# Key blocks of 96 partitions whose overlaps and memory rows all come by DMA

## The chip, the core and the metric

The kernel runs on one core of a Trainium2 chip. The metric is the device time of one execution in microseconds (us), from the first to the last instruction. Five engines work side by side and are joined by semaphores: TensorE (PE, matrix products), VectorE (DVE), ScalarE (ACT), GpSimd (POOL) and SyncE (SP, which only issues transfers). Transfers (DMA) run on 16 engines that are shared by all queues. SBUF is the on-chip memory of 128 partitions, PSUM the memory into which TensorE writes.

## The reference: what is computed

Two stages in one launch. First, chunked attention over 4 batches x 8 heads x 768 positions x 64. A chunk of 32 queries sees 16 keys to its left, its own 32 and 8 to its right, and 8 memory rows that each head has besides:

```python
chunk, left_ctx, right_ctx = (32, 16, 8)
for c in range(nc):
    c_start, c_end = c * chunk, (c + 1) * chunk          # names shortened
    l_start, r_end = max(0, c_start - left_ctx), min(S, c_end + right_ctx)
    k_full = concat([mem_k, k[:, :, l_start:r_end]])
    v_full = concat([mem_v, v[:, :, l_start:r_end]])
    a = softmax(q_c @ k_full.T / sqrt(64))
    out[:, :, c_start:c_end] = a @ v_full
```

Then, on x of shape 4 x 768 x 512 (the heads side by side):

```python
u  = x + real(fft(fft(x, axis=1), axis=2))
un = (u - mean) / sqrt(var + 1e-6)
out = u + relu(un @ w_ch1) @ w_ch2          # 512 -> 2048 -> 512
```

## The kernel before

The work is cut into 16 *pairs* of heads (n = 0 to 15), four to a batch. For each pair: q and k are loaded, cast to bf16, transposed on TensorE (trq, trk) and copied out of PSUM by ScalarE (qT, kTb); scores, exponentials and the product with v follow in two halves g. Two chunks of 32 queries are taken together, so a *block* is 64 queries wide, and a bias per half (mbias) masks the keys that a chunk must not see. The softmax needs no sum of its own: v has a 65th column of ones, and column 64 of the product is the denominator.

A block's keys span 16 + 64 + 8 rows and the 8 memory rows. Before, a block had 128 partitions: 64 keys (0 to 63), the memory rows (64 to 71), unused rows (72 to 95) and, at 96 to 127, the first 32 keys of the next block, which hold what the overlap needs. In kTb this comes for free, because blocks stand 96 columns apart and a block of 128 columns reads into the next one. For v, GpSimd copies the rows inside SBUF.

```python
    NV = 6
    va = [spool.tile([P, NB, 66], FP32, name=f"va{i}") for i in range(NV)]      # NB = 13 blocks

    def e_load_v(n, hh):                        # one head
        b, pr = seq[n]
        v1 = va[(2 * n + hh) % NV]
        vb = v[b, 2 * pr + hh]
        nc.sync.dma_start(v1[16:64, 0:NT, 0:D],                # NT = 12
                          bass.AP(tensor=vb.tensor, offset=vb.offset,
                                  ap=[[D, 48], [64 * D, NT], [1, D]]))
        nc.sync.dma_start(v1[0:16, 1:NB, 0:D],
                          bass.AP(tensor=vb.tensor, offset=vb.offset + 48 * D,
                                  ap=[[D, 16], [64 * D, NT], [1, D]]))
        nc.sync.dma_start(v1[64:72, 0:NT, 0:D],
                          mem_v[b, 2 * pr + hh].unsqueeze(1).to_broadcast([NMEM, NT, D]))

    def e_overlap(n, hh):
        v1 = va[(2 * n + hh) % NV]
        nc.gpsimd.tensor_copy(v1[96:128, 0:NT, 0:D + 1], v1[0:32, 1:NB, 0:D + 1])

    def e_kT(n):
        nc.scalar.copy(
            strided(kTb[n % NKT], 0, [[BS, NB], [8, 8], [1, RB]]),           # BS = 96
            strided(tr_of.pop((n, 1)), 0, [[8, NB], [1, 8], [KP, RB]]))      # KP = 104

    def e_scores(n, g):        # ... cut
                nc.tensor.matmul(sc[:, hh, t6, :], kT[r0:r0 + 64, t * BS:t * BS + P],
                                 qT[r0:r0 + 64, ts(t, 64)], start=True, stop=True,
                                 tile_position=(r0, 0))

    def e_exp(n, g):           # ... cut
            nc.scalar.activation(e1[:, :, :, ts(half, 32)], sc[:, :, 0:6, ts(half, 32)],
                                 AFT.Exp, bias=mbias[:, half:half + 1], scale=1.0 / math.sqrt(D))

    def e_values(n, g):        # ... cut
                    nc.tensor.matmul(xa[64 * half:64 * half + 64, st, hh, 0:65],
                                     e1[:, hh, t6, :], v1[:, 6 * g + t6, 0:65],
                                     start=True, stop=True)
```

At the start, six va, three kf and two kTb tiles are cleared: one kf on VectorE, one va and both kTb on GpSimd, the rest on ScalarE.

After the attention of a batch comes its Fourier part: sums and differences on VectorE (zy, pq, ff), a split into two fp16 halves (hi on ScalarE, lo on VectorE), products with cosine and sine tables (ps, pm), sums and statistics on VectorE. Then the MLP: ph = first matrix, hT = relu on ScalarE, pc = second matrix, osb on VectorE, and a store. The Fourier part of one batch and the attention of the next run beside the MLP of the batch before.

In which order each engine takes these steps is decided in the kernel itself, before anything is issued. A small planner (class Plan) gets every step with an engine, a guessed cost, its predecessors and the buffers that it takes and gives back, plays the schedule through with these guesses and emits the steps in the order found. A guess thus never changes what is computed, but it can change the order of the queues:

```python
        lq = add("SP", 0.35, lambda: e_load_q(n), take=("qf",), moved=1.3)
        lk = add("SP", 0.35, lambda: e_load_k(n), [t_clear["kf", n] if n < NS else None],
                 take=("kf",), moved=1.3)
        lv = [add("SP", 1.1, lambda hh=hh: e_load_v(n, hh),
                  [t_ones[2 * n + hh] if 2 * n < NV else None],
                  take=("va",) if hh == 0 else (), moved=2.3) for hh in range(2)]
        # batch 0: casts on VectorE, the others: on GpSimd
        ov = [add("POOL", 0.84, lambda hh=hh: e_overlap(n, hh), [lv[hh]]) for hh in range(2)]
        # ...
            v_ = add("PE", 0.85, lambda g=g: e_values(n, g), [x_] + ov, take=(tag,),
                     give=("e1", "va") if g == 1 else ("e1",))
```

The weights w_ch1 and w_ch2 are loaded through GpSimd's queue, in order behind its casts and copies.

Of the kernel before, what the change touches and what calls it, by code (L numbers as in the profile page):

```python
# [10 lines left out]
FP32 = mybir.dt.float32  # L11
# [6 lines left out]
LEFT = 16  # L18
RIGHT = 8
NMEM = 8  # L20
BIGM = 800.0

# [89 lines left out]
def kernel(  # L112
# [22 lines left out]
    KP = QP + 8  # L135
    NB = KP // 8
    BS = 96
# [18 lines left out]
    NV = 6  # L156
    va = [spool.tile([P, NB, 66], FP32, name=f"va{i}") for i in range(NV)]
    NKT = 2
    kTb = [spool.tile([P, NB * BS], BF16, name=f"kTb{i}") for i in range(NKT)]

    HP = H // 2
    seq = [(b, pr) for b in range(B) for pr in (0, 2, 1, 3)]

    plan = Plan(dict(qf=NS, kf=NS, va=NV // 2, kTb=NKT, qb=1, kb=1, qT=2, tr=1, sc=1, xa=1, e1=3,
# [6 lines left out]
    mkf = cpool.tile([P, 2, D], FP32)  # L171
    mkb = cpool.tile([P, 2 * D], BF16)
# [11 lines left out]
    ident = cpool.tile([P, P], FP32)  # L184
# [25 lines left out]
    def e_masks():  # L210
        nc.gpsimd.memset(mbias, NEG)
        nc.gpsimd.memset(mbias[0:72, :], 0.0)
        nc.gpsimd.memset(mbias[96:128, 1:2], 0.0)
        nc.gpsimd.affine_select(out=mbias[0:64, 0:1], in_=mbias[0:64, 0:1],
                                compare_op=ALU.is_ge, fill=NEG,
                                base=CHUNK + LEFT + RIGHT - 1, pattern=[[0, 1]],
                                channel_multiplier=-1)
        nc.gpsimd.memset(mbias[0:32, 1:2], NEG)
        nc.gpsimd.affine_select(out=mbias[96:128, 1:2], in_=mbias[96:128, 1:2],
                                compare_op=ALU.is_ge, fill=NEG, base=RIGHT + LEFT - 1,  # L220
                                pattern=[[0, 1]], channel_multiplier=-1)
# [5 lines left out]
    def e_clear_act(t):  # L227
        flat = t if len(t.shape) == 2 else t.rearrange("p a b -> p (a b)")
        nc.scalar.copy(flat, zero[0:flat.shape[0]].to_broadcast(list(flat.shape)))

    def e_ones(i):
        nc.vector.memset(va[i][0:72, :, 64:65], 1.0)
        nc.vector.memset(va[i][0:16, 0, 64:65], 0.0)
        nc.vector.memset(va[i][0:64, NB - 1, 64:65], 0.0)
        nc.vector.memset(va[i][0:16, NB - 1, 64:65], 1.0)
# [8 lines left out]
    def e_load_q(n):  # L244
        b, pr = seq[n]
        nc.sync.dma_start(qf[n % NS],
                          q[b, 2 * pr:2 * pr + 2].rearrange("h (p j) d -> p h (j d)", j=RB))

    def e_load_k(n):
        b, pr = seq[n]  # L250
        nc.sync.dma_start(kf[n % NS][2:2 + QP],
                          k[b, 2 * pr:2 * pr + 2].rearrange("h (p j) d -> p h (j d)", j=RB))

    def e_load_v(n, hh):
        b, pr = seq[n]
        v1 = va[(2 * n + hh) % NV]
        vb = v[b, 2 * pr + hh]
        nc.sync.dma_start(v1[16:64, 0:NT, 0:D],
                          bass.AP(tensor=vb.tensor, offset=vb.offset,
                                  ap=[[D, 48], [64 * D, NT], [1, D]]))  # L260
        nc.sync.dma_start(v1[0:16, 1:NB, 0:D],  # L261
                          bass.AP(tensor=vb.tensor, offset=vb.offset + 48 * D,
                                  ap=[[D, 16], [64 * D, NT], [1, D]]))
        nc.sync.dma_start(v1[64:72, 0:NT, 0:D],
                          mem_v[b, 2 * pr + hh].unsqueeze(1).to_broadcast([NMEM, NT, D]))


    qT_of, kT_of, qb_of, kb_of, tr_of, e1_of, sc_of, xa_of, xs = ({} for _ in range(9))
    cp_q = "p h (j d) -> p h j d"
    cp_b = "p j h d -> p h j d"  # L270

    def e_cast_q(n, eng):
        qb_of[n] = apool.tile([QP, RB, 2, D], BF16, tag="qb", bufs=1, name="qb")
        eng.tensor_copy(qb_of[n].rearrange(cp_b), qf[n % NS].rearrange(cp_q, j=RB))  # L274

    def e_cast_k(n, eng):
        kb_of[n] = apool.tile([KP, RB, 2, D], BF16, tag="kb", bufs=1, name="kb")
        eng.tensor_copy(kb_of[n].rearrange(cp_b), kf[n % NS].rearrange(cp_q, j=RB))

    def e_overlap(n, hh):  # L280
        v1 = va[(2 * n + hh) % NV]
        nc.gpsimd.tensor_copy(v1[96:128, 0:NT, 0:D + 1], v1[0:32, 1:NB, 0:D + 1])  # L282
# [24 lines left out]
    def e_mkT(n):  # L307
        b, pr = seq[n]
        nc.vector.tensor_copy(
            kTb[n % NKT].rearrange("p (b c) -> p b c", b=NB)[:, 0:NT, 64:72],  # L310
            mkT[:, b * HP + pr, :].unsqueeze(1).to_broadcast([P, NT, NMEM]))

    def e_kT(n):
        nc.scalar.copy(  # L314
            strided(kTb[n % NKT], 0, [[BS, NB], [8, 8], [1, RB]]),
            strided(tr_of.pop((n, 1)), 0, [[8, NB], [1, 8], [KP, RB]]))

    def e_scores(n, g):
        qT, kT = qT_of[n], kTb[n % NKT]
        sc_of[n, g] = sc = aps.tile([P, 2, 8, 64], FP32, tag="sc", bufs=1, name="sc")  # L320
        for t6 in range(6):
            t = 6 * g + t6
            for hh in range(2):
                r0 = 64 * hh
                nc.tensor.matmul(sc[:, hh, t6, :], kT[r0:r0 + 64, t * BS:t * BS + P],  # L325
                                 qT[r0:r0 + 64, ts(t, 64)], start=True, stop=True,
                                 tile_position=(r0, 0))

    def e_exp(n, g):
        sc = sc_of.pop((n, g))  # L330
        e1_of[n, g] = e1 = apool.tile([P, 2, 6, 64], FP32, tag="e1", bufs=3, name="e1")
        for half in range(2):
            nc.scalar.activation(e1[:, :, :, ts(half, 32)], sc[:, :, 0:6, ts(half, 32)],  # L333
                                 AFT.Exp, bias=mbias[:, half:half + 1],
                                 scale=1.0 / math.sqrt(D))

    def e_values(n, g):
# [6 lines left out]
        for st in range(3):  # L344
            for hh in range(2):
                v1 = va[(2 * n + hh) % NV]
                for half in range(2):
                    t6 = 2 * st + half
                    nc.tensor.matmul(xa[64 * half:64 * half + 64, st, hh, 0:65],  # L349
                                     e1[:, hh, t6, :], v1[:, 6 * g + t6, 0:65],  # L350
                                     start=True, stop=True)
# [174 lines left out]
    t_clear = {}  # L526
    t_clear["kf", 0] = add("DVE", 0.9, lambda: nc.vector.memset(kf[0], 0.0))
    t_id = add("POOL", 0.5, lambda: make_identity(nc, ident))
    t_clear["va", 0] = add("ACT", 1.0, lambda: e_clear_act(va[0]), [t_zero])
    t_clear["va", 1] = add("POOL", 0.9, lambda: nc.gpsimd.memset(va[1], 0.0))  # L530
    t_scales = add("DVE", 0.2, e_scales, [t_iota])
    t_idb = add("DVE", 0.25, lambda: nc.vector.tensor_copy(ident_b, ident), [t_id])
    t_masks = add("POOL", 0.9, e_masks)
    for i in range(1, NS):
        t_clear["kf", i] = add("ACT", 1.15, lambda i=i: e_clear_act(kf[i]), [t_zero])
        for m in (2 * i, 2 * i + 1):
            t_clear["va", m] = add("ACT", 1.0, lambda m=m: e_clear_act(va[m]), [t_zero])
    for i in range(NKT):
        t_clear["kTb", i] = add("POOL", 1.15, lambda i=i: nc.gpsimd.memset(kTb[i], 0.0))
    t_ones = {i: add("DVE", 0.3, lambda i=i: e_ones(i), [t_clear["va", i]]) for i in range(NV)}  # L540
# [27 lines left out]
    def attention(n):  # L568
        b, pr = seq[n]
        lq = add("SP", 0.35, lambda: e_load_q(n), take=("qf",), moved=1.3)  # L570
        lk = add("SP", 0.35, lambda: e_load_k(n), [t_clear["kf", n] if n < NS else None],
                 take=("kf",), moved=1.3)
        lv = [add("SP", 1.1, lambda hh=hh: e_load_v(n, hh),
                  [t_ones[2 * n + hh] if 2 * n < NV else None],
                  take=("va",) if hh == 0 else (), moved=2.3) for hh in range(2)]
        first = b == 0
        ce, cn, cc = (nc.vector, "DVE", 0.68) if first else (nc.gpsimd, "POOL", 1.04)
        cq = add(cn, cc, lambda: e_cast_q(n, ce), [lq], take=("qb",), give=("qf",))
        ck = add(cn, cc, lambda: e_cast_k(n, ce), [lk], take=("kb",), give=("kf",))
        ov = [add("POOL", 0.84, lambda hh=hh: e_overlap(n, hh), [lv[hh]]) for hh in range(2)]  # L580
# [4 lines left out]
        mk = add("DVE", 0.2, lambda: e_mkT(n), [t_mkT, t_clear["kTb", n] if n < NKT else None],  # L585
                 take=("kTb",))
        ek = add("ACT", 0.85, lambda: e_kT(n), [tk, mk], give=(ktag,))
        for g in range(2):
# [5 lines left out]
            v_ = add("PE", 0.85, lambda g=g: e_values(n, g), [x_] + ov, take=(tag,),  # L594
# [192 lines left out]
```

The softmax here doesn't subtract the row's maximum and nothing guards it: scores larger than these inputs give would overflow.

## Time and profile before

| | |
|---|---|
| time, median of 3 runs | 342.35 us (341.04 to 342.84) |
| span of the profiled execution | 339.3 us |
| moved by DMA | 33.02 MB in 51839 packets, 40032 of them under 512 bytes |
| share of GpSimd | 80.6 us busy, 24% of the span |

The profile page gives busy times by engine, the span in slices, the DMA queues, the chain of work that ended last (followed back from the last instruction to what released each step), and groups of equal instructions. In a group, "L282 POOL COPY va<-va ... x32 | 36.2, 1138 | 50.0 <-DMA" would read: line 282, on GpSimd, 32 instructions, 36.2 us in all, 1138 ns each; before them the engine stood idle for 50.0 us, most of it ended by a DMA. A table of windows gives, for each stretch of time, how long each engine was busy (with the number of instructions), the clock that TensorE was granted, the share of the 16 DMA engines' time in which packets were under way (it can pass 1, as packets overlap) and the rate in GB/s.

The DMA queue of SyncE carries the loads of q, k and v, and the transposes of un:

```
q1 hardware_dynamic: 45376, 22.03, 36.9%
```

that is packets, MB and the time of the packets as a share of 16 engines' span.

### The profile page before, as it was taken

To read this page: it belongs to the slowest core of one execution; us is meant where nothing else is said; L and a number is where in the kernel's file an instruction comes from. 1 tells how busy PE (TensorE), PEld (TensorE's weight loads), DVE (VectorE), ACT (ScalarE), POOL (GpSimd) and SP (SyncE) were. 2 spreads that over 40 slices of the span, in tenths; PEclk is the share of its full clock that TensorE was granted. 3 is DMA by queue.
4 is the path that set the end of the run, shared out by engine and by line. 5 is a ranking of instruction groups with operands and counts; after the bars stand their busy time and mean duration, and the time that the engine had idled before them with its cause. 6 is when DMAs were issued, how large, how long until landed. Compare 5 with 4: busy or idle time off the path is not lost.

```text
span 339.3 us, 6789 instructions
## 1 busy us (share of the span) xinstructions
PE 289.6 (85%) x2761; PEld 185.4 (55%) x2761; DVE 183.2 (54%) x356; ACT 168.9 (50%) x297; POOL 80.6 (24%) x89
## 2 busy tenths in 40 slices
PE   0678647969998886969999997898999999999995
PEld 0467536847565565547755654574445454554542
DVE  6964498868089899599773469782010100101001
ACT  7554885557637448676633623335436053250620
POOL 5634594224342637252001200000010000000000
PEclk9999999879999999898999999599999999999999
DMA  7999999999407785692063100000340100201001
GB/s 157 214 183 162 168 229 203 220 173 178 72 3 152 131 182 136 183 201 36 0 110 101 31 3 2 31 31 33 68 119 2 62 31 2 93 0 64 31 32 63
DMA packets 51839, 33.02 MB, mean 97 GB/s; under 512 B 40032, under 2 KB 42080, under 8 KB 51808
## 3 DMA queue, kind: packets, MB, share of 16 engines
q1 hardware_dynamic: 45376, 22.03, 36.9%
q0 software_dynamic: 2688, 4.19, 6.7%
q10 hardware_dynamic: 3744, 6.36, 4.9%
q8 instruction: 22, 0.36, 0.5%
q14 instruction: 9, 0.07, 0.1%
HBM read 28.11 MB, written 6.29 MB: 101 GB/s over the span
## 4 chain that ended last, share of the span: by engine, by line
PE 62%; DVE 14%; DMA 9%; ACT 4%; POOL 3%; issue 3%; SPq 3%; ACTq 0%; POOLq 0%
PE ph L496 23%; PE pc L510 22%; DMA qf<-in_q_dram 8%; PE xa L349 7%; PE pm L445 4%; PE ps L413 2%; SPq L261 2%; DVE zy L373 2%; DVE lo L403 2%; PE sc L325 1%; DVE ff L390 1%; DVE st L457 1%; DVE pq L381 1%; ACT e L333 1%; DVE pq L380 1%
## 5 line engine op out<-in xcount | busy, mean ns | idle before, releaser
L503 ACT ACTIVATE hT<-ph 128x384 f16<-128x384 f32 x128 | 61.2, 492 | 70.5 <-PE ph L496 70.3
L496 PE MATMUL ph<-unT,w_sb 128*128 128x384 f16 x512 | 92.2, 327 | 2.4 <-ACT hT L503 1.8
L510 PE MATMUL pc<-w_sb,hT 128*128 128x512 f16 x384 | 87.3, 382 | 0.0
L516 DVE SCALAR_TENSOR_TENSOR osb<-pc,rstd,xsb 128x512 f32<-128x512 f32 x24 | 17.8, 746 | 98.3 <-PE pc L510 98.3
L496 PEld LDWEIGHTS <-w_sb 128*128 128x128 f16 x512 | 48.3, 97 | 37.9 <-issue 8.2
L510 PEld LDWEIGHTS <-hT 128*128 128x128 f16 x384 | 37.2, 98 | 42.4 <-issue 1.5
L282 POOL COPY va<-va 32x780 f32<-32x780 f32 x32 | 36.2, 1138 | 50.0 <-DMA va<-in_v_dram 37.9
L333 ACT ACTIVATE e<-sc,mbias 128x384 f32<-128x384 f32 x64 | 33.7, 579 | 20.0 <-PE sc L325 19.1
L349 PE MATMUL xa<-va,e 128*64 128x65 f32 x768 | 35.4, 253 | 8.6 <-ACT e L333 3.7
L349 PEld LDWEIGHTS xa<-va,e 128*64 128x64 f32 x768 | 30.6, 162 | 15.7 <-issue 7.7
L463 ACT ACTIVATE un<-xsb,mu_s 128x512 f16<-128x512 f32 x24 | 17.3, 722 | 24.5 <-DVE mu_s L458 15.8
L359 DVE RECIPROCAL zs<-xa 128x6 f32<-128x6 f32 x32 | 6.1, 190 | 34.5 <-PE xa L349 34.3
L325 PE MATMUL sc<-qT,kTb 64*128 64x64 bf16 x384 | 12.8, 207 | 12.6 <-ACT kTb L314 11.0
L484 POOL TENSOR_SCALAR rstd<-mu_s 128x6 f32<-128x6 f32 x4 | 1.0, 244 | 89.7 <-DVE osb L516 83.7
L413 PE MATMUL ps<-cosS,lo 128*128 128x193 f16 (+1 forms) x72 | 16.6, 285 | 4.6 <-DVE lo L403 4.5
L274 POOL CAST qb<-qf 96x1024 bf16<-96x1024 f32 x12 | 14.9, 1242 | 20.8 <-DMA qf<-in_q_dram 11.9
L413 PE MATMUL ps<-cosS,hi 128*128 128x193 f16 (+1 forms) x72 | 16.7, 285 | 3.4 <-DVE ff L390 3.2
L425 ACT CAST up<-ps 128x386 f16<-128x386 f32 x16 | 9.7, 605 | 19.4 <-PE ps L413 17.8
L325 PEld LDWEIGHTS <-kTb 64*128 64x128 bf16 x384 | 8.8, 104 | 18.5 <-ACT kTb L314 12.3
L360 DVE TENSOR_TENSOR xsb<-xa,zs 128x384 f32<-128x384 f32 x32 | 17.8, 557 | 1.1
L398 ACT CAST hi<-ff 128x768 f16<-128x768 f32 x16 | 13.2, 832 | 10.1 <-DVE ff L390 9.9
L403 DVE TENSOR_TENSOR lo<-ff,hi 128x768 f16<-128x768 f32 x16 | 16.8, 1063 | 2.2 <-ACT hi L398 2.1
(90 smaller groups left out, 356.2 us busy)
## 6 DMA issues: line engine op xcount, KB each, us to landing
qf<-in_q_dram SPq DMA_DIRECT2D x16, 384.0 KB
kf<-in_k_dram SPq DMA_DIRECT2D x16, 384.0 KB
out_dram<-osb ACTq DMA_DIRECT2D x24, 256.0 KB, 2.0
va<-in_v_dram SPq DMA_DIRECT2D x32, 144.0 KB, 5.8
w_sb<-in_moe_w_ch_dram POOLq DMA_DIRECT2D x8, 512.0 KB, 16.1
va<-in_v_dram SPq DMA_DIRECT2D x32, 48.0 KB, 6.8
va<-in_mem_v_dram SPq DMA_DIRECT2D x32, 24.0 KB
unT<-un SPq DMA_TRANSPOSE x18, 2.4
```

The source lines that it names most:

```text
L282: nc.gpsimd.tensor_copy(v1[96:128, 0:NT, 0:D + 1], v1[0:32, 1:NB, 0:D + 1])
L325: nc.tensor.matmul(sc[:, hh, t6, :], kT[r0:r0 + 64, t * BS:t * BS + P], qT[r0:r0 + 64, ts(t, 64)], start=True, stop=True, tile_position=(r ...
L333: nc.scalar.activation(e1[:, :, :, ts(half, 32)], sc[:, :, 0:6, ts(half, 32)], AFT.Exp, bias=mbias[:, half:half + 1], scale=1.0 / math.sqr ...
L349: nc.tensor.matmul(xa[64 * half:64 * half + 64, st, hh, 0:65], e1[:, hh, t6, :], v1[:, 6 * g + t6, 0:65], start=True, stop=True)
L360: nc.vector.tensor_tensor(xs[b][:, 3 * g:3 * g + 3, 2 * pr * D:(2 * pr + 2) * D] .rearrange("p s (h d) -> p s h d", h=2), xa[:, :, :, 0:D] ...
L403: nc.vector.tensor_tensor(lo[:, ab].rearrange(fl), ff_of[b, par][:, ab].rearrange(fl), hi[:, ab].rearrange(fl), ALU.subtract)
L413: nc.tensor.matmul(out_[:, sp, :], part[:, ab, sp * 3 + st, c0:c1], tab[:, sp, st, :], start=(st == 0 and i == 0), stop=(st == 2 and i == 1))
L463: nc.scalar.activation(un, xs[b][:, kt, :], AFT.Identity, bias=mu_of[b][:, kt, 0:1], scale=-1.0)
L496: nc.tensor.matmul(ph[:, 0:384], w1_sb[:, dt, ts(ht, P)], unT_of[b][:, dt, sh * 384:(sh + 1) * 384], start=(dt == 0), stop=(dt == NDT - 1))
L503: nc.scalar.activation(hT_of[b, sh][:, ht, :], ph_of.pop((b, sh, ht))[:, 0:384], AFT.Relu, bias=0.0, scale=-1.0)
L510: nc.tensor.matmul(pc_of[b, sh, stl], hT_of[b, sh][:, ht, ts(stl, P)], w2_sb[:, ht, :], start=(ht == 0), stop=(ht == NHT - 1))
L516: nc.vector.scalar_tensor_tensor(osb, pc_of.pop((b, sh, stl)), rstd_of[b][:, st:st + 1], xs[b][:, st, :], ALU.mult, ALU.add)
```

## The change

A block now has 96 partitions: 8 memory rows (0 to 7), 16 keys to the left (8 to 23), the 64 own keys (24 to 87) and 8 to the right (88 to 95). v is loaded into that layout completely, with keys that two blocks need read twice from HBM, so that the copies on GpSimd go[...]. kTb gets the same layout, with its overlap made by ScalarE's copy out of PSUM (12 x 88 columns in place of 13 x 64), and its gaps need no clearing. One va tile holds both heads of a pair. k needs two rows of padding at either end, which are cleared alone. At the two ends of the sequence, keys that don't exist are zeros with a zero in the ones column (e_edges, e_edge_ones). Some small constants share a buffer with osb, and the planner's guesses are new, with v at 2.6 for the transfer of a pair.

```diff
+OWN = NMEM + LEFT
+WIN = OWN + 64 + RIGHT
-    KP = QP + 8
-    NB = KP // 8
-    BS = 96
+    KP = QP + 4
+    KOFF = LEFT // RB
-    NV = 6
-    va = [spool.tile([P, NB, 66], FP32, name=f"va{i}") for i in range(NV)]
+    NV = 3
+    va = [spool.tile([WIN, 2, NT, 66], FP32, name=f"va{i}") for i in range(NV)]
-    kTb = [spool.tile([P, NB * BS], BF16, name=f"kTb{i}") for i in range(NKT)]
+    kTb = [spool.tile([P, NT, WIN], BF16, name=f"kTb{i}") for i in range(NKT)]
 ...   masks: the same keys hidden in the new layout
-    def e_clear_act(t):
-        flat = t if len(t.shape) == 2 else t.rearrange("p a b -> p (a b)")
-        nc.scalar.copy(flat, zero[0:flat.shape[0]].to_broadcast(list(flat.shape)))
+    def e_edges(i):
+        v1 = va[i]
+        nc.vector.memset(v1[:, :, :, D:D + 1], 1.0)
+        nc.vector.memset(v1[0:32, :, 0, 0:D], 0.0)
+        nc.vector.memset(v1[64:WIN, :, NT - 1, 0:D], 0.0)
 ...   e_edge_ones: two affine_select and a memset on GpSimd for each va tile
 ...   e_kzero: 2 and 4 rows of each kf tile
-        nc.sync.dma_start(v1[16:64, 0:NT, 0:D], ...)
-        nc.sync.dma_start(v1[0:16, 1:NB, 0:D], ...)
-        nc.sync.dma_start(v1[64:72, 0:NT, 0:D], ...)
-    def e_overlap(n, hh):
-        v1 = va[(2 * n + hh) % NV]
-        nc.gpsimd.tensor_copy(v1[96:128, 0:NT, 0:D + 1], v1[0:32, 1:NB, 0:D + 1])
+        def run(p0, count, t0, nt, key, hh):
+            vb = v[b, 2 * pr + hh]
+            nc.sync.dma_start(v1[p0:p0 + count, hh, t0:t0 + nt, 0:D],
+                              bass.AP(tensor=vb.tensor, offset=vb.offset + key * D,
+                                      ap=[[D, count], [64 * D, nt], [1, D]]))
+        nc.sync.dma_start(v1[OWN:OWN + 64, :, 0, 0:D],
+                          v[b, 2 * pr:2 * pr + 2, 0:64].rearrange("h p d -> p h d"))
+        for hh in range(2):
+            run(NMEM, OWN - NMEM + 64, 1, NT - 1, 64 - LEFT, hh)
+            run(OWN + 64, RIGHT, 0, NT - 1, 64, hh)
+            nc.sync.dma_start(v1[0:NMEM, hh, :, 0:D],
+                              mem_v[b, 2 * pr + hh].unsqueeze(1).to_broadcast([NMEM, NT, D]))
-            strided(kTb[n % NKT], 0, [[BS, NB], [8, 8], [1, RB]]),
-            strided(tr_of.pop((n, 1)), 0, [[8, NB], [1, 8], [KP, RB]]))
+            strided(kTb[n % NKT], NMEM, [[WIN, NT], [RB, 11], [1, RB]]),
+            strided(tr_of.pop((n, 1)), 0, [[64 // RB, NT], [1, 11], [KP, RB]]))
-                nc.tensor.matmul(sc[:, hh, t6, :], kT[r0:r0 + 64, t * BS:t * BS + P],
+                nc.tensor.matmul(sc[0:WIN, hh, t6, :], kT[r0:r0 + 64, t, :],
-        lv = [add("SP", 1.1, lambda hh=hh: e_load_v(n, hh), ..., moved=2.3) for hh in range(2)]
+        lv = add("SP", 2.8, lambda: e_load_v(n), ..., take=("va",), moved=2.6)
-        ov = [add("POOL", 0.84, lambda hh=hh: e_overlap(n, hh), [lv[hh]]) for hh in range(2)]
-        ek = add("ACT", 0.85, lambda: e_kT(n), [tk, mk], give=(ktag,))
+        ek = add("ACT", 1.0, lambda: e_kT(n), [tk, mk], give=(ktag,))
-            v_ = add("PE", 0.85, lambda g=g: e_values(n, g), [x_] + ov, take=(tag,),
+            v_ = add("PE", 0.85, lambda g=g: e_values(n, g), [x_, lv], take=(tag,),
```

## The prediction

> **What bounds the kernel now.** I began with the busy times, then cut the span into stages, because the 85% of TensorE is an average.
>
> ```profile
> PE 289.6 (85%) x2761; PEld 185.4 (55%) x2761; DVE 183.2 (54%) x356; ACT 168.9 (50%) x297; POOL 80.6 (24%) x89
> ```
>
> ```profile
> core 0: us, PE busy (x) PEld busy (x) DVE busy (x) ACT busy (x) POOL busy (x), PEclk, DMA share, GB/s
> 0.00:20.00 20.00, 7.62 (x105) 6.10 (x105) 16.92 (x58) 12.45 (x16) 11.69 (x21) 1.00 1.00 183
> 20.00:40.00 20.00, 16.52 (x264) 14.13 (x264) 7.62 (x19) 11.64 (x20) 7.78 (x8) 1.00 1.16 177
> 40.00:77.00 37.00, 24.47 (x327) 20.18 (x328) 31.40 (x63) 23.99 (x38) 19.68 (x18) 0.91 1.13 202
> 77.00:100.00 23.00, 22.78 (x259) 13.97 (x257) 12.47 (x23) 14.35 (x27) 10.73 (x11) 1.00 0.51 86
> 100.00:160.00 60.00, 48.99 (x682) 35.44 (x681) 53.65 (x89) 37.10 (x65) 25.74 (x25) 0.94 0.73 145
> 160.00:182.00 22.00, 21.54 (x149) 13.72 (x148) 14.79 (x29) 9.72 (x17) 0.00 (x0) 1.00 0.30 60
> 182.00:340.00 158.00, 147.70 (x981) 81.84 (x979) 46.31 (x81) 59.68 (x118) 5.01 (x6) 0.98 0.13 40
> ```
>
> The cuts are events of the trace: 40 is the end of batch 0's attention, 77 the first MLP matmul (ph), 182 the first ph of batch 1. TensorE is idle 20.0 - 7.6 + 20.0 - 16.5 = 15.9 us before 40, 12.5 from 40 to 77, 11.7 from 77 to 182, 10.3 after that (0.7 of it behind the end). GpSimd, whose copies go, has nothing to do after 160 but two short rstd steps and the last two copies.
>
> Next, the chain of waits in order of time, at places that name what the stages wait for:
>
> ```profile
> 9.32 1.70 POOL va L282
> ...
> 13.62 1.57 PE xa L349 x24
> ...
> 32.79 7.19 DMA qf<-in_q_dram
> ...
> 57.05 14.37 DMA qf<-in_q_dram
> ...
> 92.14 0.85 PE xa L349 x24
> ...
> 104.71 4.47 DMA qf<-in_q_dram
> ```
>
> An overlap copy is on the chain once, 1.70 us. The same values matmuls take 1.57 us at 13.6 and 0.85 at 92: early TensorE work costs nearly double, so most of the chain between 12 and 32 is slow TensorE and exponentials, not loads. Between 33 and 72 it hangs on loads of q, in a stage where the DMA share is over 1.
>
> Last, the groups and waits of the copies:
>
> ```profile
> L282 POOL COPY va<-va 32x780 f32<-32x780 f32 x32 | 36.2, 1138 | 50.0 <-DMA va<-in_v_dram 37.9
> L314 ACT COPY kTb<-trk 128x832 bf16<-128x832 bf16 x16 | 13.7, 854 | 5.6 <-PE trk L304 4.6 <-POOL va L282 0.9
> ```
>
> ```profile
> L309 DVE COPY kTb<-mkT x16: 174/279/869, 8.6 to 148.8; 128x96 bf16<-128x96 bf16 x16
> ...
> L389 DVE COPY ff<-pq x16: 153/171/1008, 43.8 to 211.9; 128x6 f32<-128x6 f32 x16
> ...
> L381 DVE TENSOR_TENSOR pq<-zy x8: 944/950/1596, 42.9 to 209.6; 128x768 f32<-128x768 f32 x8
> ```
>
> ```profile
> SPq L261 <- DMA out_dram<-osb: 20.0, 2, 19.5
> ```
>
> The copies are 36.2 of GpSimd's 80.6 us, and it stood 37.9 us at their head waiting for v, with the casts of q and k queued behind. In the second block (min/median/max) the same VectorE instruction takes five to six times as long at worst for the two short ones. The last line is SyncE holding up a v load for 19.5 us until an output store had landed.
>
> [...]944 ns at the fastest, 1596 at the slowest for line 381.
> [...]all that shows is 177 to 202 GB/s with the engines' share over 1.
> [...]
>
> **The change part by part.**
> *GpSimd.* 32 copies go: -36.2 us busy. It gains nine short edge operations and five small zeroings of kf before 10 us, and loses kTb and va clears there (2.2 + 0.8 us). Its casts no longer stand behind a copy that waits for v.
> *VectorE.* Excess over the fastest case: line 309 (391 - 174) x 16 = 3.5 us, line 389 (413 - 153) x 16 = 4.2, line 403 (1063 - 882) x 16 = 2.9, lines 380, 381 and 373 together 3.6; 14.2 us. The copies are 36.2 of 36.2 + 14.9 + 13.0 us of large GpSimd work, 56%: about 8 us of VectorE come back. Only where VectorE sets the pace (100 to 160) does this show: 9.7 of the 36.2 us of copies lie there, so some 2 us.
> *ScalarE.* Seven clears go, 4.3 + 2.1 = 6.4 us before 10 us. kT grows from 832 to 1056 elements; q's copy of 768 takes 800 ns, that of 832 takes 854, so 0.84 ns an element and 1.04 us: +0.19 x 16 = +3.0 us, spread over 150 us, on an engine half idle.
> *TensorE.* Same instructions; score outputs have 96 rows, which changes no column count. k's transposes lose 4 of 104 columns. Zero.
> *DMA.* Runs of 256 bytes per pair: before 2 x (576 + 192 + 96) = 1728; after 128 + 2 x (880 + 88 + 96) = 2256, +31% or +135 KB. With 768 KB of q and k the pair grows 11%. At the 181 GB/s of the stage this is +0.75 us a pair[...]. The first v load no longer waits for the 0.9 us ScalarE clear (issued at 4.28), so it starts 1.5 to 2 us earlier. SyncE issues 9 transfers a pair instead of 8, and each waits for the eighth before it.
> *Order.* The kernel's own planner, which was given new costs, reorders the queues. I compared TensorE's two instruction lists: from batch 1's first ph on (182 us) they are the same. Before it, q transposes of pairs 8, 9 and 10 come 8 to 12 us of TensorE work earlier among the ph of batch 0, where before 48 ph matmuls stood in one block and the Fourier work of batch 1 and 2 came late. In the waits of the new program, the first SyncE load that waits for an output store is q of pair 12, not v of pair 9.
>
> **Sum.**
> 0 to 40: the scores of pair 0 need k through VectorE's cast (9.30) and ScalarE (11.02 after a 0.91 wait). Without contention about 0.7 us earlier; without copies and slowed VectorE casts in pairs 1 and 2, another 1.3. -2.
> 40 to 77: stays on loads and weights, whose 16.1 us to landing do not change. A GpSimd free of 7.5 us of copies: -1, and more v bytes +0.
> 77 to 182: 105 us that hold 93.3 us of TensorE. The 11.7 idle lie where VectorE is 89% busy while it was only 54% busy from 77 to 100. The earlier attention moves that work forward, and the 2 us of contention go. I take 5 of the 11.7: -5.
> 182 to the end: the same instructions, no copies on the path: 0.
> 342.35 - 8 = 334 us.
>
> **Rivals.**
> 1. *The loads become the bound.* More runs, two narrow transfers a head, and a planner that assumes them faster than I can show: it allows 2.6 us for a pair's v where it allowed 4.6. If v costs 31% more, about 1 us a pair, pairs 0 to 8 arrive up to 9 us late in all; loads led their use by some 5 us in pair 3 (v copied at 28.7 to 31.5, used at 35.2), which eats part. TensorE would then stand at q of pairs 8 to 10. For it: DMA share over 1 to 77. Against it: 0.51 from 77 to 100. It makes 338 to 346.
> 2. *Wider spread makes loads faster.* [...]b0 and the weights finish earlier, and 40 to 77 shrinks by 4 to 6 us: 326 to 330.
> 3. *The copies were hidden anyway.* Only 1.70 us of them stand on the chain, and the Fourier chain on VectorE in 100 to 160 stays as long. Gain 1 to 3 us: 339 to 341.
>
> **Range and chances.** Between rival 2 and the middle of rival 1: 325 to 343. The limit for over 2% faster is 335.5, just above my number; I give faster 0.55, within 2% 0.37, slower 0.08, the last for rival 1 with stalls in TensorE's fixed order.
>
> **What would show it.** Right: GpSimd near 45 us busy; the mean of line 309's and 389's counterparts nearer 0.2 us; end of batch 0's attention near 38, first ph near 74, batch 1's first ph near 174, and 157 us from there. SyncE's 19.5 us wait gone or moved to pair 12. Wrong: if the first ph comes later than 77 (rival 1) or before 71 (rival 2); if TensorE's q transposes of pairs 8 to 10 wait for casts for more than 3 us; if 77 to 182 stays near 105 with VectorE as busy as before (rival 3); or if the part after batch 1's first ph differs from 157 by over 2 us.

## Result and the profile after

The new kernel took 336.79 us (median of 4 runs, 336.54 to 337.84) against 342.60 (341.04 to 343.16): ratio 0.984, 95% interval 0.980 to 0.988. Measured once more beside later experiments it was 338.98 against 342.74, ratio 0.991 (0.987 to 0.995). Both intervals lie below 1: a gain of 5.8 us by the first medians and 3.8 by the second. Predicted were 8 (334.0), with a range of 325 to 343, and over 2% faster was given a chance of 0.55: both gains, 1.6% and 0.9%, are below 2%.

The busy times of the page of the new kernel:

```profile
PE 289.2 (86%) x2761; PEld 187.1 (56%) x2761; DVE 177.3 (53%) x341; ACT 164.6 (49%) x290; POOL 48.9 (15%) x66
```

GpSimd lost 31.7 us of work, VectorE 5.9, ScalarE 4.3. TensorE lost nothing, although its granted clock was higher (0.982 over the span, 0.969 before). The time fell by less than a fifth of what GpSimd shed.

The table of windows with the cuts of the prediction (us busy of each engine, clock, share of the DMA engines, GB/s):

```profile
0.00:20.00 20.00, 7.51 (x103) 6.25 (x104) 15.12 (x42) 5.89 (x8) 8.68 (x26) 1.00 1.03 192
20.00:40.00 20.00, 14.07 (x208) 12.02 (x206) 7.13 (x16) 9.48 (x15) 2.54 (x3) 1.00 1.06 197
40.00:77.00 37.00, 26.54 (x354) 22.18 (x351) 29.47 (x61) 26.68 (x42) 11.09 (x13) 0.95 1.11 211
77.00:100.00 23.00, 22.11 (x358) 15.71 (x359) 18.09 (x38) 17.49 (x32) 8.84 (x9) 1.00 0.89 166
100.00:160.00 60.00, 53.83 (x661) 38.76 (x662) 51.19 (x88) 38.48 (x66) 14.60 (x13) 0.97 0.70 133
```

From 20 to 40 TensorE does *less* than before (14.1 us, was 16.5): the first stage got worse. From 77 to 100 VectorE does more (18.1, was 12.5), and from 100 to 160 TensorE does more (53.8, was 49.0): that is where the time came from. More of the attention's short matmuls lie in 77 to 100 (TensorE has 358 instructions there, before 259), and more of the MLP's long ones behind it (661 take 53.8 us, before 682 took 49.0).

To see this without fixed cuts, I read four events from the timelines of each kernel: the first score matmul, the end of batch 0's attention (its eighth xsb), the first ph, and batch 1's first ph. They carry the reading of all experiments, so all are in one table (us; the profiled execution of each). Some executions are slowed as a whole: the ratios of this text leave them out, its medians do not, and e7, whose profiled execution was one of them, is not in the table.

| | first scores | attention 0 ends | first ph | batch 1's first ph | end | between the last two ph |
|---|---|---|---|---|---|---|
| before | 11.92 | 40.78 | 76.58 | 181.25 | 339.3 | 104.7 |
| after | 12.85 | 46.65 | 78.72 | 177.61 | 334.8 | 98.9 |
| after, second time (e10) | 11.87 | 47.88 | 79.23 | 178.47 | 337.0 | 99.2 |
| e1 before, no copies | 11.41 | 40.52 | 76.82 | 180.68 | 338.6 | 103.9 |
| e2 before, other guess | 12.04 | 47.61 | 79.90 | 180.89 | 339.0 | 101.0 |
| e3 after, 128 columns | 12.91 | 46.47 | 78.30 | 175.84 | 333.4 | 97.5 |
| e4 after, guess 4.0 | 12.85 | 42.52 | 77.69 | 175.36 | 332.7 | 97.7 |
| e5 both | 11.92 | 41.17 | 76.56 | 171.10 | 328.1 | 94.5 |
| e9 both, second time | 12.85 | 41.22 | 76.69 | 174.27 | 331.3 | 97.6 |
| e6 both, zeroing moved | 10.66 | 42.00 | 77.63 | 174.92 | 332.0 | 97.3 |
| e8 after, fewer loads | 12.85 | 46.00 | 78.58 | 176.26 | 334.4 | 97.7 |
| e11 both, fewer loads | 11.93 | 41.60 | 75.35 | 172.60 | 329.3 | 97.3 |
| e12 before, v in other rows | 12.43 | 41.18 | 77.22 | 180.88 | 337.6 | 103.7 |

So the new kernel loses 2.1 us up to the first ph, gains 5.8 between the two ph, and 0.9 behind. Rows of one and the same kernel (after and e10, e5 and e9) differ by up to 1.2 us in the early events and 3.2 us in the late ones; smaller differences of single rows say nothing. The 0.93 us by which the first scores come later after the change are such a case: in e10 they come at 11.87, before its 11.92.

Why the first stage is longer stands in the timeline of TensorE of the new kernel (start, length, line, operation; in brackets the idle time before it and who ended it):

```profile
19.58 0.85 PE L305 MATMUL trk<-ident_b,kb 100*128 100x100 bf16 x8
21.13 0.82 PE L289 MATMUL trq<-ident_b,qb 96*128 96x96 bf16 x8 [0.71 <-DVE qb L262]
21.89 0.69 PE L326 MATMUL sc<-qT,kTb 64*96 64x64 bf16 x12
...
27.78 0.85 PE L305 MATMUL trk<-ident_b,kb 100*128 100x100 bf16 x8 [0.90 <-DVE kb L262]
28.56 1.57 PE L350 MATMUL xa<-va,e 96*64 96x65 f32 x24
...
33.33 0.82 PE L289 MATMUL trq<-ident_b,qb 96*128 96x96 bf16 x8 [2.58 <-POOL qb L262]
34.08 1.57 PE L350 MATMUL xa<-va,e 96*64 96x65 f32 x24
```

The trq at 33.33 belongs to the fifth pair, of batch 1, whose q GpSimd casts; it stands in the queue *ahead* of a values matmul (34.08) whose data are there, and TensorE waits 2.58 us for the cast. The same place in the timeline of the kernel before has the order turned round, and no cast on the way:

```profile
31.94 1.57 PE L349 MATMUL xa<-va,e 128*64 128x65 f32 x24 [1.21 <-ACT e L333]
33.45 0.50 PE L325 MATMUL sc<-qT,kTb 64*128 64x64 bf16 x12
33.88 0.82 PE L288 MATMUL trq<-ident_b,qb 96*128 96x96 bf16 x8
35.16 1.57 PE L349 MATMUL xa<-va,e 128*64 128x65 f32 x24 [0.46 <-ACT e L333]
```

In the new kernel TensorE idles 0.71 + 0.90 + 2.58 = 4.2 us at transposes that wait for casts; before, none does between 12 and 41 us. The cast at the longest of these waits had itself waited for its load, as the chain of waits of the new kernel shows:

```profile
27.23 4.85 DMA qf<-in_q_dram
...
32.26 1.03 POOL qb L262
...
33.33 0.82 PE trq L289 x8
```

So the order makes TensorE wait there for a load that ready work need not have waited for. The second thing to see is the length of a group of twelve score matmuls: 0.69 us against 0.50.

The short VectorE instructions that the prediction named (min/median/max in ns), three answers about one line each:

```profile
L310 DVE COPY kTb<-mkT x16: 168/180/1015, 9.2 to 155.4; 128x96 bf16<-128x96 bf16 x16
L390 DVE COPY ff<-pq x16: 102/166/1007, 50.2 to 208.6; 128x6 f32<-128x6 f32 x16
L382 DVE TENSOR_TENSOR pq<-zy x8: 943/950/1789, 49.3 to 206.3; 128x768 f32<-128x768 f32 x8
```

The medians of the first two fell from 279 and 171 to 180 and 166 ns, but the worst cases of all three stayed: GpSimd still has the casts of q and k, which lie beside the long cases of the last two (at 139.99 and 104.63 us; casts at 139.37 for 1.60 us and at 104.54 for 1.06), and the new zeroings, which lie beside that of the first (at 9.2 us; zeroings from 5.55 to 10.24). And SyncE's wait for an output store went from 19.5 to 9.1 us, now at a load of q or k instead of v:

```profile
SPq L256 <- DMA out_dram<-osb: 9.1, 1, 9.1
```

### The profile page after: what moved, and what is told of

Its sections match the earlier page's. It is cut to its first block, busy times and chain, and to the rows that moved or that the text cites. A ratio compares the mean times of both kernels' runs of the same rounds, so it can differ in the third digit from the quotient of the medians.

```text
span 334.8 us, 6729 instructions
## 1 busy us (share of the span) xinstructions
PE 289.2 (86%) x2761; PEld 187.1 (56%) x2761; DVE 177.3 (53%) x341; ACT 164.6 (49%) x290; POOL 48.9 (15%) x66
## 4 chain that ended last, share of the span: by engine, by line
PE 68%; DVE 16%; ACT 7%; DMA 4%; issue 1%; SPq 1%; POOL 0%; ACTq 0%; POOLq 0%; DVEq 0%
PE pc L511 24%; PE ph L497 22%; PE xa L350 7%; PE ps L414 6%; PE pm L446 4%; ACT e L334 3%; PE sc L326 2%; DVE ff L391 2%; DVE lo L404 2%; DVE zy L374 2%; DMA mkf<-in_mem_k_dram 1%; DMA qf<-in_q_dram 1%; DMA unT<-un 1%; DVE xsb L361 1%; DVE pq L381 1%
## 5 line engine op out<-in xcount | busy, mean ns | idle before, releaser
L511 PE MATMUL pc<-w_sb,hT 128*128 128x512 f16 x384 | 85.8, 379 | 0.0
L334 ACT ACTIVATE e<-sc,mbias 96x384 f32<-96x384 f32 x64 | 33.4, 571 | 22.2 <-PE sc L326 21.5
L350 PE MATMUL xa<-va,e 96*64 96x65 f32 x768 | 35.3, 252 | 10.2 <-ACT e L334 9.4
L350 PEld LDWEIGHTS xa<-va,e 96*64 96x64 f32 x768 | 30.4, 162 | 17.4 <-ACT e L334 10.4
L326 PE MATMUL sc<-qT,kTb 64*96 64x64 bf16 x384 | 16.9, 228 | 3.8 <-ACT kTb L315 2.0
L326 PEld LDWEIGHTS <-kTb 64*96 64x96 bf16 x384 | 13.2, 141 | 9.8 <-issue 4.7
L315 ACT COPY kTb<-trk 128x1056 bf16<-128x1056 bf16 x16 | 16.6, 1036 | 3.7 <-PE trk L305 3.7
L374 DVE TENSOR_TENSOR zy<-xsb 128x768 f32<-128x768 f32 x16 | 17.4, 1098 | 0.3
L414 PEld LDWEIGHTS <-lo 128*128 128x128 f16 (+1 forms) x120 | 13.3, 110 | 7.2 <-DVE lo L404 6.4
L452 DVE TENSOR_TENSOR xsb<-pm,xsb 128x512 f32<-128x512 f32 x24 | 16.0, 667 | 2.2 <-PE pm L446 2.2
```

What stands on the lines that cost most here:

```text
L315: nc.scalar.copy(strided(kTb[n % NKT], NMEM, [[WIN, NT], [RB, 11], [1, RB]]), strided(tr_of.pop((n, 1)), 0, [[64 // RB, NT], [1, 11], [KP, ...
L326: nc.tensor.matmul(sc[0:WIN, hh, t6, :], kT[r0:r0 + 64, t, :], qT[r0:r0 + 64, ts(t, 64)], start=True, stop=True, tile_position=(r0, 0))
L334: nc.scalar.activation(e1[:, :, :, ts(half, 32)], sc[0:WIN, :, 0:6, ts(half, 32)], AFT.Exp, bias=mbias[0:WIN, half:half + 1], scale=1.0 / ...
L374: nc.vector.tensor_tensor(zy_of[b, par][:, :, c0:c0 + P], xb[:, :, c0:c0 + P], xb[:, :, HD + c0:HD + c0 + P], ALU.add if par == 0 else ALU ...
L414: nc.tensor.matmul(out_[:, sp, :], part[:, ab, sp * 3 + st, c0:c1], tab[:, sp, st, :], start=(st == 0 and i == 0), stop=(st == 2 and i == 1))
L511: nc.tensor.matmul(pc_of[b, sh, stl], hT_of[b, sh][:, ht, ts(stl, P)], w2_sb[:, ht, :], start=(ht == 0), stop=(ht == NHT - 1))
```

## The experiments

My theory after this reading had three parts: the gain comes partly from the missing copies and partly from TensorE's new order from the first ph on; the same order costs time before the first ph; and score weights of 96 columns cost TensorE time. The rivals were loads that had become the bound (the prediction's rival 1), and for each part that it did nothing.

Where an experiment leaves something out of the computation, it is said.

**e1: the kernel before without its copies.** The planner's step stays and emits nothing, so every other engine keeps its order. The keys of the overlap are missing from the output.

```diff
-        ov = [add("POOL", 0.84, lambda hh=hh: e_overlap(n, hh), [lv[hh]]) for hh in range(2)]
+        ov = [add("POOL", 0.84, lambda: None, [lv[hh]]) for hh in range(2)]
```

> The kernel before with its 32 overlap copies left out and nothing else: the planner still counts them, so that all queues keep their order (rows 96 to 127 of v stay zero, so the overlap keys are missing from the output). Copies theory (the gain came from GpSimd's copies): about the new kernel's time, 337 us, with VectorE 6 us less busy. Order theory (the gain came from the new order that the planner found): 341 to 343 us, for the copies were hidden; VectorE is still some 4 to 8 us less busy.

340.19 against 343.43 us, ratio 0.991 (0.988 to 0.995): between the two expectations. The page's busy times:

```profile
PE 290.0 (86%) x2761; PEld 185.8 (55%) x2761; DVE 176.3 (52%) x356; ACT 168.6 (50%) x297; POOL 46.2 (14%) x57
```

VectorE lost 183.2 - 176.3 = 6.9 us with none of its work removed: that is what the copies had held it up, some 19% of their 36.2 us. It shows in single lines: without the copies the mean of line 381 is 951 ns in place of 1108, that of the short lines 309 and 389 is 268 and 320 ns in place of 391 and 413. By what the two engines hold each other up is not shown. About 3 us reach the end. (The profiled execution of e1 was granted 0.934 of TensorE's clock, that of before 0.969, so e1's row in the table is not a measure of this gain.)

**e2: the kernel before, with only the planner's guess changed.** Nothing is computed or moved otherwise; the copies stay.

```diff
-                  take=("va",) if hh == 0 else (), moved=2.3) for hh in range(2)]
+                  take=("va",) if hh == 0 else (), moved=1.3) for hh in range(2)]
```

> The kernel before with one number changed: the planner's guess for the transfer of a head's v, 2.3 to 1.3, which gives a pair the 2.6 of the new kernel; copies and layout stay. Order theory: 336 to 339 us; batch 0's attention ends later than before (46 us as in the new kernel, against 40), but batch 1's first ph comes near 179 us against 182. Copies theory: 341 to 345 us, for GpSimd's copies stand in the way of an order that is tighter.

340.12 us, ratio 0.993 (0.990 to 0.996): 1 us above the range of the order theory, and below that of the other. The row of e2 in the table repeats the shape of the new kernel: the attention of batch 0 ends late, at 47.61, and the stretch between the two ph is short, 101.0. TensorE's timeline there:

```profile
27.27 0.82 PE L288 MATMUL trq<-ident_b,qb 96*128 96x96 bf16 x8 [1.85 <-DVE qb L274]
29.66 0.88 PE L304 MATMUL trk<-ident_b,kb 104*128 104x104 bf16 x8 [1.56 <-DVE kb L278]
...
34.81 0.82 PE L288 MATMUL trq<-ident_b,qb 96*128 96x96 bf16 x8 [2.35 <-POOL qb L274]
```

The same stalls at transposes that wait for casts, with the old loads, the old layout and the copies in place. So the late attention comes from the order. The stretch between the two ph is 104.7 - 101.0 = 3.7 us shorter, little more than the 3.1 by which e5 and e9, one kernel, differ in it; but the work has moved as in the new kernel (VectorE is 17.6 us busy from 77 to 100, before 12.5, after 18.1):

```profile
77.00:100.00 23.00, 21.11 (x348) 14.82 (x345) 17.60 (x39) 18.44 (x35) 12.15 (x13) 1.00 0.81 145
```

The gains of e1 and e2 (3.0 and 2.4 us by their ratios) add to 5.4, about what the whole change brought in its first measurement and more than in its second.

**e3: the new kernel with score weights of 128 columns.** kTb gets 32 columns of zeros behind it, and each block's weights read 32 columns into the next block. The product gets 32 rows that nobody reads.

```diff
-    kTb = [spool.tile([P, NT, WIN], BF16, name=f"kTb{i}") for i in range(NKT)]
+    kTp = [spool.tile([P, NT * WIN + 32], BF16, name=f"kTb{i}") for i in range(NKT)]
+    kTb = [t[:, 0:NT * WIN].rearrange("p (t w) -> p t w", t=NT) for t in kTp]
-                nc.tensor.matmul(sc[0:WIN, hh, t6, :], kT[r0:r0 + 64, t, :],
+                nc.tensor.matmul(sc[:, hh, t6, :], kT[r0:r0 + 64, t * WIN:t * WIN + P],
```

> The new kernel, but the scores' weight loads take 128 columns again (96 of the block and 32 of the next one, whose scores nobody reads). Weight theory (a load of 96 columns is slower than one of 128): a group of 12 score matmuls falls from 0.69 to 0.50 us at the start and TensorE's busy time by 4 us; 333 to 334.5 us if most of it is on the path, as TensorE is the bound for most of the span. Rival (the time of a score matmul comes from elsewhere, such as the 96 rows that it writes, or it is hidden): 336 to 337 us.

335.5 us, ratio 0.983 (0.975 to 0.991), between the two expectations. The groups of the score matmuls and their weight loads, for the kernel before, the new one and e3:

```profile
L325 PE MATMUL sc<-qT,kTb 64*128 64x64 bf16 x384 | 12.8, 207 | 12.6 <-ACT kTb L314 11.0 <-ACT e L333 1.5
L325 PEld LDWEIGHTS <-kTb 64*128 64x128 bf16 x384 | 8.8, 104 | 18.5 <-ACT kTb L314 12.3 <-issue 4.5 <-ACT un L463 0.2
```

```profile
L326 PE MATMUL sc<-qT,kTb 64*96 64x64 bf16 x384 | 16.9, 228 | 3.8 <-ACT kTb L315 2.0 <-ACT e L334 1.7
L326 PEld LDWEIGHTS <-kTb 64*96 64x96 bf16 x384 | 13.2, 141 | 9.8 <-issue 4.7 <-ACT kTb L315 3.4
```

```profile
L329 PE MATMUL sc<-qT,kTb 64*128 64x64 bf16 x384 | 12.7, 206 | 4.1 <-ACT kTb L318 2.3 <-ACT e L337 1.8
L329 PEld LDWEIGHTS <-kTb 64*128 64x128 bf16 x384 | 8.6, 103 | 10.0 <-issue 4.8 <-ACT kTb L318 3.5
```

Here fewer columns load more slowly: 141 ns for 96, 103 for 128, and with 128 the scores are back at 12.7 us. TensorE's busy time fell from 289.2 to 284.5 at the same granted clock (0.982 and 0.983). In the time of the whole kernel the step is small: 336.8 to 335.5, and less by the ratios to the kernel before, 0.984 and 0.983. It is shown for TensorE and not for the end.

**e4: the new kernel with a guess of 4.0 for v.**

```diff
-                  take=("va",), moved=2.6)
+                  take=("va",), moved=4.0)
```

> The new kernel with one number changed: the planner's guess for a pair's v transfer 2.6 to 4.0, so that TensorE meets pair 4's q transpose after pair 2's values and not before them. Order theory: batch 0's attention ends at 41 to 43 us in place of 46, and the time falls to 332 to 335 us if the middle keeps its gain. Rival (the first 46 us are held by the loads themselves, not by the order): the end of batch 0's attention stays within 1 us and the time is 336 to 339 us.

333.92 us, ratio 0.976 (0.969 to 0.983). The attention ends at 42.52 instead of 46.65. The place in TensorE's timeline where the trq of the fifth pair had blocked:

```profile
33.34 1.57 PE L350 MATMUL xa<-va,e 96*64 96x65 f32 x24 [1.20 <-ACT e L334]
34.84 0.69 PE L326 MATMUL sc<-qT,kTb 64*96 64x64 bf16 x12
35.46 0.82 PE L289 MATMUL trq<-ident_b,qb 96*128 96x96 bf16 x8
```

The values go first, and the transpose finds its cast done. A planner told that v takes longer plans later work later; the loads themselves are the same. The stretch between the two ph stays short (97.7). In the time, the intervals of e4 and of the new kernel just overlap, so that e4 alone makes its 2 to 3 us likely; e9 and e10 below compare both edits on one chip.

**e5: both edits.**

> The new kernel with two edits together: the score weights are 128 columns of a padded kTb instead of 96, and the planner's guess for a pair's v is 4.0 instead of 2.6. Alone they gave 335.5 and 333.9 against 336.8 for the new kernel. Theory (two separate costs, one of TensorE work and one of order): both gains add, 336.8 - 1.3 - 2.9 = about 332.6, TensorE 284 to 285 us busy, end of batch 0's attention near 42.3. Rival (both shorten the same stretch up to 46 us): no better than the better one alone, 333.5 to 334.5.

330.9 us, ratio 0.972 (0.965 to 0.979), below both expectations; repeated as e9.

**e6: besides, the zeroing of the k edges of two tiles on ScalarE.** GpSimd's four zeroings become four ScalarE copies of zeros.

```diff
-                   add("POOL", 0.9, lambda i=i: e_kzero(i, 1, nc.gpsimd), rank=17),
+                   add("ACT", 1.04, lambda i=i: e_kzero_act(i, 1), [t_zero]),
```

> As the run before, and besides the zeroing of the k edges of the second and third kf tile goes from GpSimd to ScalarE, which is idle then. Theory (four GpSimd zeroings of 1.2 us lie on top of VectorE's first casts and stretch them from 0.68 to 1.2 and 1.5 us): the first scores start near 12.0 instead of 12.85, and half or more of that reaches the end: 331.7 to 332.3. Rival (the casts wait for the loads of q and k, or the start is absorbed later because the first ph hangs on the loads of the weights): the first scores may move, the time stays within 0.4 us of the run before.

333.22 us, ratio 0.978 (0.971 to 0.985): no gain over e5 or e9. The transposes behind VectorE's first casts of q and k came at 7.89 and 8.68 us, in e5, where these casts took 1.18 and 1.45 us, at 8.39 and 9.94, and the first scores came at 10.66, earlier than in any other kernel. The chain of waits shows where that went:

```profile
7.62 6.79 DMA kf<-in_k_dram
...
14.84 6.36 DMA kf<-in_k_dram
...
21.74 6.70 DMA kf<-in_k_dram
28.46 0.70 DVE kb L270
```

The k loads of the second, third and fourth pair follow one another, and the fourth k lands at 28.4, no sooner than without this edit (27.6 in e5). The rival's reason held; its number, 0.4 us from the run before, did not (333.2 against 330.9), though it fits e9 (333.0).

**e7: the kernel before, copies to rows that no product reads.** The 32 copies keep size and source; their target is 32 rows added to a qf tile. TensorE's order is that of before. The overlap keys are missing from the output.

```diff
-        nc.gpsimd.tensor_copy(v1[96:128, 0:NT, 0:D + 1], v1[0:32, 1:NB, 0:D + 1])
+        nc.gpsimd.tensor_copy(vx[:, :, 0:D + 1], v1[0:32, 1:NB, 0:D + 1])
```

> The kernel before in its order; its 32 overlap copies stay, same size and source, but write to unused rows of a wider qf tile, so that no product with v waits for them (the overlap keys are missing from the output). Without any copies the time was 340.2 against 343.4. Theory A (what the copies cost is their hold on VectorE and on the casts behind them in GpSimd's queue): the time stays at the time before, within 0.8 us, with VectorE 182 to 184 us busy. Theory B (what they cost is TensorE waiting for the copied rows): 340 to 341, like the run without copies, though VectorE stays at 182 to 184.

341.35 against 342.42 us, ratio 0.997 (0.994 to 1.000): between the two expectations, and nearer to A. Of the 0.9% that e1 gained, a third is left when only TensorE's wait for the rows goes. This speaks for their hold on VectorE and GpSimd's queue as the larger part of their cost, but the intervals of e1 and e7 overlap at their ends, and the shares are not settled.

**e8: the new kernel without the narrow loads from the fourth pair on.** Memory rows and right overlap of v are stale in the output. (The share in the expectation is miswritten: it is 368 of the 2256 runs of a pair's v, 16%.)

```diff
         for hh in range(2):
             run(NMEM, OWN - NMEM + 64, 1, NT - 1, 64 - LEFT, hh)
+            if n >= NV:
+                continue
```

> The new kernel, but from the fourth pair on the four transfers of 8 partitions (memory rows and right overlap of v) are left out, so those rows are stale; that takes 40 of 256 kB-runs a hundred out of v's share, about 17% of v's runs. Theory (the longer first stage comes from the order of TensorE's queue, not from the loads): the end of batch 0's attention moves by less than 1 us from 46.65, and the time by less than 1 us from 336.8. Rival (the loads of v, or their narrow transfers, bind up to 46 us): the loads of q come sooner by 0.5 us or more a pair, the end of the attention falls to 42 to 44.5, and the time to 332 to 335.

336.03 us, ratio 0.987 (0.980 to 0.993); attention ends at 46.00 instead of 46.65. Within 1 us on both, as the order predicts. The q of the fifth pair was issued at 24.0 instead of 27.2, and the wait of its transpose went from 2.58 only to 2.16 us. The edit leaves the loads of the first three pairs, and k of the fourth, as they were, so it speaks of the loads behind them only.

**e9, e10: the fastest version and the new kernel once more, on the same chip.**

> The fastest version so far (128 columns of score weights, guess 4.0) once more, beside the new kernel on the same chip, because its 330.9 lay 1.7 below the sum of its two parts and its interval is 1.4% wide. Theory (the parts add, and the rest was spread between executions): 332 to 333, 4 to 5 less than the new kernel in the next run. Rival (the two edits help each other): 330 to 331.5.

> The new kernel unchanged, as the measure for the run before: 336.8 by its first times, 336 to 338 now, ratio to the kernel before 0.980 to 0.988.

e9: 332.99 us, ratio 0.971 (0.966 to 0.975). e10: 338.98, ratio 0.991 (0.987 to 0.995), above what I expected of it. The version with both edits is 6.0 us faster than the new kernel here, and the intervals lie apart: shown. By ratio e5 and e9 agree (0.972 and 0.971), so 2.8 to 2.9% is the number to keep for it; that the median was 330.9 in e5 and 333.0 here is no gain of one over the other.

**e11: the fastest version without the narrow loads from the fourth pair on.** Output as in e8.

> The fastest version, and from the fourth pair on the transfers of 8 partitions (memory rows and right overlap of v) left out, so those rows are stale. In the new kernel leaving them out moved the end of batch 0's attention by 0.65 us only, because TensorE's order came last there. In the fastest version the chain of waits up to 41 us hangs on loads of v and k again. Theory (with the order mended, the loads bind): the end of the attention falls from 41.2 to 38 to 39.5, as 84 of a hundred of v's runs of 256 bytes are left, and the time by 1 to 3 us. Rival (the first 41 us are slow TensorE and exponentials, not loads): less than 0.7 us on either.

334.17 us, ratio 0.975 (0.970 to 0.980): no gain over e9. Yet the loads did come sooner: q of the seventh pair was issued at 36.96, in e9 at 41.94. Five us on the loads moved the end of the attention by +0.4, the first ph by -1.3 and the time by nothing. These loads don't set the time, even in the version whose order is mended. For the first four pairs this isn't shown: the chain of e5 hangs on loads from 9 to 28 us, that of e9, the same kernel, on TensorE, so the two are about equally long there, and no run makes those loads faster in this version.

```profile
8.90 5.91 DMA va<-in_v_dram
...
14.87 6.03 DMA va<-in_v_dram
...
20.96 6.65 DMA kf<-in_k_dram
```

**e12: the kernel before, v in other rows.** The transfers keep their sizes; the output is another one.

```diff
-        nc.sync.dma_start(v1[16:64, 0:NT, 0:D],
+        nc.sync.dma_start(v1[48:96, 0:NT, 0:D],
-        nc.sync.dma_start(v1[64:72, 0:NT, 0:D],
+        nc.sync.dma_start(v1[16:24, 0:NT, 0:D],
```

> The kernel before in its order; the same transfers of v with the same sizes land in other rows: the 48 rows of own keys in 48 to 95 instead of 16 to 63, the memory rows in 16 to 23 instead of 64 to 71 (the output is thereby another one). In the window from 12 to 41 us the kernel before moved 175 GB/s and the new one 197. Theory (the rate rose because v is spread over more of the 128 partitions): 183 to 195 GB/s here, the end of batch 0's attention 1 us earlier or more, 338 to 341. Rival (the rate rose for another reason, such as fewer and larger transfers, or because more was waiting to be moved): 172 to 179 GB/s, time within 1 us of before.

338.78 us, ratio 0.987 (0.981 to 0.993). The window from 12 to 41 us of the kernel before, of the new one, and of e12 (the last two numbers are the share of the DMA engines and GB/s):

```profile
12.00:41.00 29.00, 22.07 (x352) 18.77 (x352) 16.48 (x36) 16.20 (x27) 12.84 (x11) 1.00 1.20 175
```

```profile
12.00:41.00 29.00, 20.21 (x294) 17.28 (x296) 14.23 (x31) 14.05 (x23) 3.54 (x4) 1.00 1.09 197
```

```profile
12.00:41.00 29.00, 22.04 (x352) 18.91 (x352) 16.65 (x36) 16.17 (x27) 15.88 (x16) 1.00 1.14 196
```

With the same transfers in other rows the rate rises to that of the new kernel: 12% from the rows alone. The kernels with v in the old rows moved 171 (e2) to 177 GB/s (e1) in this window. Even the 48 KB transfers of v, whose rows stay, land sooner in this window: 5.8 us after their issue (median), before 7.0. v takes 72 rows as before, only others; why these let the rate rise, no view here shows. But the end of the attention, which the theory had tied to the rate, did not follow (41.18, was 40.78): the chain of waits in e12 runs from 12 to 40 through TensorE and ScalarE alone. Why the time still fell by about 4 us isn't shown; its profiled execution is 1.7 us shorter than that of before, of which 0.4 lie ahead of batch 1's first ph. It stays open. The rows are thus a third source of gain beside the copies and the order: alone these bring 4.4, 3.0 and 2.4 us by their ratios (e12, e1, e2), more together than the 3.8 to 5.8 of the whole change. So the gains overlap, or the new kernel loses part of them elsewhere, and the share of each in it is not shown.

## Why the prediction was right in its total and wrong in its steps

The time fell inside the range, by 5.8 and 3.8 us in place of 8. That says little for the reasoning: the range of 18 us held 342.6, no gain at all, too, and the right side of zero was reached although the first two steps, -3 together, came out as +2.1. Of the steps:

- *0 to 40: -2.* **This step failed.** The end of the attention moved from 40.78 to 46.65 and 47.88, +5.9 and +7.1. I had compared TensorE's two lists, reported pairs 8 to 10, and took the first 40 us as if their order had not changed. It had: transposes of later pairs stand ahead of ready work and wait for casts (4.2 us, in e10 6.7), which e2 reproduces with nothing but a guess and e4 undoes with one (42.52). The narrower score weights take 8 x 0.19 = 1.5 us more of TensorE here; given up alone they brought the end of the attention 0.2 us forward (e3), and 1.3 once the order was mended (e4 to e5).
- *40 to 77: -1.* The stretch from the end of the attention to the first ph shrank by 3.7, but only because the former had moved: in e2 it shrank by 3.5 too. The first ph came 2.1 us later.
- *77 to 182: -5.* Measured -5.8 and -5.4: right in size. The mechanism was the one stated first, earlier attention that moves VectorE's work into its idle time behind 77 (18.1 us of VectorE from 77 to 100, was 12.5); order alone gives 3.7 (e2), and what the missing copies give here, where I had put 2 for contention, is open: e1's 0.8 is less than the spread of one kernel. The q transposes of pairs 8, 9 and 10 came 6 to 12 us earlier, and none of them waited for a cast. TensorE's clock from 100 to 160 was 0.97, before 0.94; in e12 it was 1.00 and the stretch still took 103.7, so the clock is not what shortened it.
- *182 to the end: 0.* Measured -0.9 and +0.5. Right.
- *TensorE: zero.* **Wrong.** I counted columns of the output and forgot those of the weights: +37 ns on each of 384 loads, which overlap one another (384 x 141 ns is 54.1 us, done in 13.2 us of busy time), so that the scores took TensorE 16.9 us in place of 12.8 (e3: 12.7). Why 96 columns take longer to load than 128 is not shown. That the number of instructions was the same said nothing about their length.
- *VectorE: 8 us back.* Measured 5.9, and 6.9 in e1. Mechanism right, term somewhat too large; that the share of copies in GpSimd's large work overstated their share in the collisions is likely and not shown. (In the kernel before, the worst case of the second short line was 6.6 times its fastest, 1008 against 153 ns, not five to six.) The means of the two short lines came down to 237 and 279 ns, not to 200: long cases are left in both (up to 1015 and 1007 ns), and those two lie beside a zeroing and a cast on GpSimd.
- *ScalarE: kT at 1.04 us.* Measured 1.036. *GpSimd near 45.* Measured 48.9; the five small zeroings, of two or four rows, are the mis-sized term: each takes 0.94 us or more.
- *DMA: +0.75 us a pair.* Not there: q of the seventh pair was issued at 41.39, before at 40.04, so 1.35 us over six pairs in place of 4.5. By e12 the other rows can have paid for the added runs. **Rival 2** was thus right about the rate (e12); its 326 to 330 did not come, and how much of the gain is due to the rows is open. **Rival 1** saw half of what happened: its sign, a first ph later than 77, came (78.7), and so did stalls in TensorE's fixed order behind a planner that takes v to be faster (e2, e4), only at the third to fifth pair (n = 2 to 4) and not at n = 8 to 10. What didn't come is its price of 1 us a pair, and sooner loads from the fourth pair on did not remove the stalls (e8). **Rival 3** gave the whole change 1 to 3 us, since the copies were hidden; e1 measured 3 for the copies alone.

## What to carry to other kernels

When a change also changes a scheduler's costs, run the old kernel with only the new costs before judging the change: here a single guess was worth 2 to 3 us (e2, and likely e4), about as much as all the removed copies (e1). Compare the order of the bounding engine from its first instruction, and ask of every instruction that stands ahead of ready work what it waits for. If weights get narrower, look at the duration of the weight load (here 141 ns in place of 104) and not only at the number of matmuls; padding them to 128 columns gave TensorE 4.7 us back here.

## What was unexpected of the hardware

A bf16 weight load of 96 columns took 141 ns and one of 128 columns 104. Moving 48 rows of a load from partitions 16 to 63 to 48 to 95, and its memory rows from 64 to 71 to 16 to 23, raised the rate of the whole stage from 175 to 196 GB/s. And zeroing a few rows cost as much here as zeroing all: in the new kernel a memset of 2 rows takes VectorE 912 ns, in the kernel before that of 104 rows took the same.

```profile
L241 POOL MEMSET kf<- x5: 942/946/1493, 0.8 to 8.7; 4x1024 f32 x3, 2x1024 f32 x2
L241 DVE MEMSET kf<- x1: 912/912/912, 1.1 to 1.1; 2x1024 f32 x1
```

```profile
L527 DVE MEMSET kf<- 104x1024 f32 x1 | 0.9, 912 | 0.2 <-issue 0.2
```
